# Sliding-window attention and channel mix: contiguous q/k evacuation, batch 0 attention pipelined, batch 1 attention inside tile 0

## The chip, the cores and the metric

One core of one Trainium2 chip. Times are device microseconds (us) of whole executions. A profiled execution has its own span, about 2 us under the time. Stages are compared in the profiled executions, totals in the timed ones.

Engines: PE is the matmul engine, PEld its weight loads, DVE the vector engine, ACT the scalar engine, POOL the general engine that here issues the loads. PSUM is the memory into which this kernel has PE write its results (the pools with `space=PS`); copying a result out of it is its evacuation. The identity is the matrix that the PE transposes of this kernel take as an operand. "L184" is line 184 of the kernel of that run.

## The reference, cut to what matters

```python
# q, k, v: (batch 8, heads 8, seq 576, dim 64), fp32
# heads 0-3: causal window of 32; heads 4-7: causal window of 128, every 4th position
scores = where(mask, q @ k^T / 8, -1e9); attn = softmax(scores); a = attn @ v
x = a as (8, 576, 512)                      # heads side by side
x_prev = x shifted by one position
xk = mu_k * x + (1 - mu_k) * x_prev;  xr = mu_r * x + (1 - mu_r) * x_prev
k = relu(xk @ w_k)                          # 512 -> 1024
out = sigmoid(xr @ w_r) * ((k * k) @ w_v)   # 1024 -> 512
```

## The kernel before: the parts that matter

The work per batch is: load, transpose q and k on PE (six steps `step_T`, each evacuated from PSUM by ACT), six attention blocks (`step_S` scores and exp, `step_P` weighted values and normalisation, `step_X` transposes of the result), then the "lerps" on DVE that make `xk` and `xr`. The dense part runs in nine tiles of 512 rows, each of 20 groups: 8 K, 4 R, 8 halves of V.

The plain heads' evacuation puts four interleaved phases r into one row, so it writes every fourth fp16 element:

```python
p_xo = ctx.enter_context(tc.tile_pool(name="p_xo", bufs=1, space=PS))   # one buffer
p_tb = ctx.enter_context(tc.tile_pool(name="p_tb", bufs=1, space=PS))   # one buffer

def step_T(b, n):
    ...
    if g == 0:      # plain heads: QKp
        for wi, w in enumerate(ws):
            o = QKp[b % 2][:, w, :, PAD:].rearrange("p h (j r) -> p h r j", r=R)[:, :, :, j0:j0 + nj]
            nc.scalar.activation(out=o, in_=tv[:, wi].rearrange("p (h r) x -> p h r x", h=2), func=AF.Copy)
    else:           # dilated heads: QKd, rows written contiguously
        ...
```

`step_T` 0 to 3 handle 96 rows (two of them plain, 128x768 each); steps 4 and 5 handle 48 rows (two 128x384 evacuations each).

The order of work, with the schedule of PE, ACT, DVE and POOL fixed by hand:

```python
load_batch(0)
make_identity(nc, ident)
... # weights w_k, w_r, w_v
load_batch(1)
...
for n in range(6): step_T(0, n)
fix_v(0)                                   # DVE copies 32 halo rows of v
for i in range(NB):                        # batch 0, block after block
    step_S(0, i); step_P(0, i, 0); step_P(0, i, 1)
    if i % 2 == 1: step_X(0, i // 2)
step_lerp_d(0); step_lerp(0, 0); step_lerp(0, 1)
scale_wv()                                 # DVE scales the value weights
for tt in range(NTT):
    if tt + 2 < B: load_batch(tt + 2)
    gs = moe_groups(tt)
    plan = attn_plan(tt + 1)               # S, P, X, lerps of batch tt+1, T of batch tt+2
    if tt == 0: plan = {}
    for g, f in enumerate(gs):             # a group, then the steps planned at it
        f()
        for a in plan.get(g, []): a()
    if tt == 0:                            # tile 0: batch 1 comes after the dense part
        for n in range(6): step_T(1, n)
        fix_v(1)
        plan = attn_plan(1)
        for g in range(20):
            for a in plan.get(g, []): a()
```

In `attn_plan`, S of block i stands at group 2i, its two P at 2i+2 and 2i+3, X after every second block, the lerps at 15, 16 and 18, the next transposes at 5, 9, 13, 15, 17 and 18, and `fix_v` at 19.

The softmax here doesn't subtract the row's maximum and nothing guards it: scores larger than these inputs give would overflow.

Of the kernel before, what the change touches and what calls it, by code (L numbers as in the profile page):

```python
# [10 lines left out]
AF = mybir.ActivationFunctionType  # L11
# [5 lines left out]
def kernel(  # L17
# [12 lines left out]
    nc = tc.nc  # L30
    B, H, S, D = q.shape
# [13 lines left out]
    lerp_p = ctx.enter_context(tc.tile_pool(name="lerp_p", bufs=1))  # L45
    xkp = ctx.enter_context(tc.tile_pool(name="xkp", bufs=3))
    k2p = ctx.enter_context(tc.tile_pool(name="k2p", bufs=2))
    outp = ctx.enter_context(tc.tile_pool(name="outp", bufs=3))
    PS = bass.MemoryType.PSUM
    p_mm = ctx.enter_context(tc.tile_pool(name="p_mm", bufs=4, space=PS))  # L50
    p_ps = ctx.enter_context(tc.tile_pool(name="p_ps", bufs=1, space=PS))
# [42 lines left out]
    def load_batch(b):  # L94
        for jc in range(2):
            load_qk(b, jc)
        load_v(b)

    ident = const.tile([128, 128], FP16)
    load_batch(0)  # L100
    make_identity(nc, ident)
    for i in range(2):
        nc.vector.memset(QKp[i][:, :, :, 0:PAD], 0.0)
        nc.vector.memset(QKd[i][:, :, :, 0:PAD], 0.0)
# [43 lines left out]
        nc.gpsimd.dma_start(out=wk[:, c], in_=moe_w_k[c * 128:(c + 1) * 128, :])  # L148
    for c in range(4):
        nc.gpsimd.dma_start(out=wr[:, c], in_=moe_w_r[c * 128:(c + 1) * 128, :])  # L150
    for c in range(8):
        nc.gpsimd.dma_start(out=wv[:, c], in_=moe_w_v[c * 128:(c + 1) * 128, :])
    load_batch(1)

    def scale_wv():
        for c in range(8):
# [5 lines left out]
    def step_T(b, n):  # L162
        jc, g, w1 = T_STEPS[n]
        j0, nj = JC[jc]
        t = ld[(b, jc)]
        tb = p_tb.tile([128, 768], FP16, name="tb")
        ws = (0, 1) if w1 is None else (w1,)
        nw = len(ws)
        tv = tb.rearrange("p (w s x) -> p w s x", w=nw, s=8)
        for wi, w in enumerate(ws):  # L170
            for sl in range(8):
                if g == 0:
                    hp, r = sl // 4, sl % 4
                    for par in range(2):
                        nc.tensor.transpose(out=tv[par * D:(par + 1) * D, wi, sl, :],  # L175
                                            in_=t[:nj, w, 2 * hp + par, r * D:(r + 1) * D], identity=ident[:nj, :nj])
                else:
                    h, rp = sl // 2, sl % 2
                    nc.tensor.transpose(out=tv[:, wi, sl, :], in_=t[:nj, w, 4 + h, rp * 2 * D:(rp + 1) * 2 * D],  # L179
                                        identity=ident[:nj, :nj])  # L180
        if g == 0:
            for wi, w in enumerate(ws):
                o = QKp[b % 2][:, w, :, PAD:].rearrange("p h (j r) -> p h r j", r=R)[:, :, :, j0:j0 + nj]
                nc.scalar.activation(out=o, in_=tv[:, wi].rearrange("p (h r) x -> p h r x", h=2), func=AF.Copy)  # L184
        else:
            for wi, w in enumerate(ws):
                o = QKd[b % 2][:, w, :, PAD:].rearrange("p h (a j) -> p h a j", a=2)[:, :, :, j0:j0 + nj]
                nc.scalar.activation(out=o, in_=tv[:, wi].rearrange("p (h a) x -> p h a x", h=4), func=AF.Copy)  # L188
# [4 lines left out]
    def step_S(b, i):  # L193
        ps = p_ps.tile([128, 2, 512], FP32, name="ps")
        for sl in range(4):
            for par in range(2):
                ho = par * 64
                if sl < 2:
                    lhsT = QKp[b % 2][ho:ho + 64, 1, sl, QB * i:QB * i + 128]
                    rhs = QKp[b % 2][ho:ho + 64, 0, sl, PAD + QB * i:PAD + QB * (i + 1)]  # L200
                else:
                    h, ii = 2 * (i % 2) + sl - 2, i // 2
                    lhsT = QKd[b % 2][ho:ho + 64, 1, h, QB * ii:QB * ii + 128]
                    rhs = QKd[b % 2][ho:ho + 64, 0, h, PAD + QB * ii:PAD + QB * (ii + 1)]
                nc.tensor.matmul(out=ps[:, par, sl * QB:(sl + 1) * QB], lhsT=lhsT, rhs=rhs, start=True, stop=True)  # L205
        at = AT[at_n[0] % 3]
        at_n[0] += 1
        nc.scalar.activation(out=at[:, :, :, 0:QB],  # L208
                             in_=ps[:, :, 0:4 * QB].rearrange("p a (s x) -> p a s x", s=4),
                             func=AF.Exp, scale=0.125)  # L210
        nc.vector.tensor_tensor(out=at[:, :, :, 0:QB], in0=at[:, :, :, 0:QB], in1=MK[combos[i]], op=ALU.mult)  # L211
        at_of[(b, i)] = at

    def step_P(b, i, g):
        at = at_of[(b, i)]
        rec = xp.tile([128, 4], FP32, name=f"rec{g}")
        x16 = xp.tile([128, 4, D], FP16, name=f"x16{g}", bufs=4)
        xo_of[(b, i, g)] = x16
        if g == 0:
            xo = p_xo.tile([128, 4, D + 1], FP32, name="xo")  # L220
            for hl in range(4):
                nc.tensor.matmul(out=xo[:, hl], lhsT=at[:, hl % 2, hl // 2, :], rhs=VAp[b % 2][:, i, hl, :],  # L222
                                 start=True, stop=True)
            nc.vector.reciprocal(out=rec[:QB], in_=xo[:QB, :, D])
            nc.vector.tensor_tensor(out=x16[:QB], in0=xo[:QB, :, 0:D],
                                    in1=rec[:QB].unsqueeze(2).to_broadcast([QB, 4, D]), op=ALU.mult)
        else:

            xo = p_xo.tile([128, 2, 2 * D + 2], FP32, name="xo")
            for hl in range(2):  # L230
                for par in range(2):
                    o = (2 * (i % 2) + hl) * (2 * D + 1) + par * (D + 1)
                    nc.tensor.matmul(out=xo[:, hl, par * (D + 1):(par + 1) * (D + 1)], lhsT=at[:, par, 2 + hl, :],
                                     rhs=VAd[b % 2][:, i // 2, o:o + D + 1], start=True, stop=True)
            rv = rec.rearrange("p (h a) -> p h a", h=2)
            nc.vector.reciprocal(out=rv[:QB], in_=xo[:QB, :, 0:2 * D + 2:2 * D + 1])
            nc.vector.tensor_tensor(out=x16[:QB].rearrange("p (a h) d -> p h a d", a=2),  # L237
                                    in0=xo[:QB, :, 1:2 * D + 1].rearrange("p h (a d) -> p h a d", a=2),
                                    in1=rv[:QB].unsqueeze(3).to_broadcast([QB, 2, 2, D]), op=ALU.mult)
# [32 lines left out]
    def step_lerp_d(b):  # L272
        xT = xT_of[b]
        dx = lerp_p.tile([128, 4, S], FP16, name="dx")
        nc.vector.tensor_tensor(out=dx[:, :, J:S], in0=xT[:, :, J:S], in1=xT[:, :, 0:S - J], op=ALU.subtract)
        nc.vector.tensor_tensor(out=dx[:, :, 1:J], in0=xT[:, :, 1:J], in1=xT[:, :, 3 * J:S - 1], op=ALU.subtract)
        nc.vector.tensor_copy(out=dx[:, :, 0:1], in_=xT[:, :, 0:1])
        xT_of[(b, "dx")] = dx
# [64 lines left out]
            gs.append(lambda ts=ts: step_V(tt, ts, 1))  # L343
        return gs

    def attn_plan(b):
        plan = {}
        if b >= B:
            return plan

        def at(g, f):
            plan.setdefault(g, []).append(f)
        for i in range(NB):
            at(2 * i, lambda i=i: step_S(b, i))
            at(2 * i + 2, lambda i=i: step_P(b, i, 0))
            at(2 * i + 3, lambda i=i: step_P(b, i, 1))
            if i % 2 == 1:
                at(2 * i + 4, lambda i=i: step_X(b, i // 2))
        at(15, lambda: step_lerp_d(b))
        at(16, lambda: step_lerp(b, 0))  # L360
        at(18, lambda: step_lerp(b, 1))
        if b + 1 < B:
            for n, g in enumerate((5, 9, 13, 15, 17, 18)):
                at(g, lambda n=n: step_T(b + 1, n))
            at(19, lambda: fix_v(b + 1))
        return plan

    with tc.manual_schedule(engines={ET.PE, ET.Activation, ET.DVE, ET.Pool}):
        for n in range(6):
            step_T(0, n)  # L370
        fix_v(0)
        for i in range(NB):
            step_S(0, i)
            step_P(0, i, 0)
            step_P(0, i, 1)
            if i % 2 == 1:
                step_X(0, i // 2)
        step_lerp_d(0)
        step_lerp(0, 0)
        step_lerp(0, 1)  # L380
        scale_wv()
        for tt in range(NTT):
            if tt + 2 < B:
                load_batch(tt + 2)
            gs = moe_groups(tt)
            plan = attn_plan(tt + 1)
            if tt == 0:
                plan = {}
            for g, f in enumerate(gs):
                f()  # L390
                for a in plan.get(g, []):
                    a()
            if tt == 0:
                for n in range(6):
                    step_T(1, n)
                fix_v(1)
                plan = attn_plan(1)
                for g in range(20):
                    for a in plan.get(g, []):
                        a()  # L400


# [28 lines left out]
```

## Time and profile before

353.17 us, median of 2 runs (352.47 to 353.86). The span of the profiled run is 351.4 us.

| stage (first K matmul to first K matmul) | us |
|---|---|
| prologue, to the first K matmul of tile 0 | 57.07 |
| tile 0 with batch 1 attention and transposes of batches 1 and 2 | 62.40 |
| tiles 1 to 6 | 192.21 |
| tiles 7 and 8 (dense only) | 39.72 |

The page of the kernel before, part 2: each digit is the busy share of one of 40 equal slices in tenths; PEclk is the granted PE clock in tenths.

```profile
span 351.4 us, 6171 instructions
...
PE   0134435973444697978788788878877977999994
...
ACT  6352331536453567567756757676677566425441
...
PEclk9999999996555589999999999999999999999999
```

PE is thin twice: in the first seven slices, and again from the tenth to the fourteenth, after the dense burst of tile 0. In the second gap its clock falls too. The table by stage for the kernel before says the same in numbers (columns: window, length, busy us and instruction count of each engine, granted clock, DMA share, GB/s); the third line is the stage with the transposes and attention of batch 1 and the transposes of batch 2 and no dense work, the last one a steady tile:

```profile
core 0: us, PE busy (x) PEld busy (x) DVE busy (x) ACT busy (x) POOL busy (x), PEclk, DMA share, GB/s
0.00:57.07 57.07, 14.91 (x217) 10.98 (x218) 22.44 (x87) 22.05 (x30) 35.69 (x63) 1.00 1.51 140
57.07:75.50 18.43, 18.43 (x78) 8.04 (x78) 9.84 (x23) 7.06 (x12) 0.00 (x0) 1.00 0.10 32
75.50:119.47 43.97, 19.19 (x316) 15.17 (x314) 16.97 (x40) 22.56 (x27) 9.69 (x14) 0.56 0.50 59
119.47:311.68 192.21, 159.72 (x1682) 81.12 (x1681) 136.84 (x317) 124.85 (x192) 31.04 (x46) 0.98 0.46 68
...
190.53:223.15 32.62, 26.68 (x297) 13.83 (x297) 23.24 (x54) 21.97 (x34) 8.14 (x12) 1.00 0.60 82
```

The evacuations of the transpose tile in the kernel before (smallest, median and largest duration in ns; first and last start; the shapes):

```profile
L184 ACT ACTIVATE QKp<-tb x32: 1023/1499/1878, 14.6 to 281.9; 128x768 f16<-128x768 f16 x16, 128x384 f16<-128x384 f16 x16
L188 ACT ACTIVATE QKd<-tb x32: 484/652/812, 20.2 to 284.1; 128x768 f16<-128x768 f16 x16, 128x384 f16<-128x384 f16 x16
L258 ACT ACTIVATE xT<-tb x24: 491/491/492, 35.0 to 307.0; 128x384 f16<-128x384 f16 x24
```

L184 and L188 move the same sizes; the strided one takes 1878 ns for what takes the other 812. L258 reads PSUM in steps of four elements and writes contiguously, and is as fast as a contiguous copy.

Who waited (us in total, times, longest), the kernel before:

```profile
PE tb L179 <- ACT QKp L184: 14.9, 10, 2.0
PE tb L253 <- ACT QKp L184: 13.9, 12, 2.0
PE tb L175 <- POOL ident masks.py:199: 13.7, 1, 13.7
...
PE tb L175 <- ACT QKp L184: 3.9, 2, 2.0
```

And where these waits sit in a steady tile: those of PE's instructions that waited for the evacuation or the mask, in order of time (start, duration, in brackets the idle time before and what ended it; three waits of 0.5 to 0.8 us for DVE's normalisation are cut). One period runs from the first line to the last.

```profile
190.51 0.30 PE L222 MATMUL xo<-VAp,AT 128*128 128x65 f16 x4 [0.81 <-DVE AT L211]
...
197.85 0.20 PE L253 MATMUL tb<-ident,x 96*128 96x96 f16 x1 [1.00 <-ACT QKp L184]
...
205.62 0.20 PE L253 MATMUL tb<-ident,x 96*128 96x96 f16 x1 [1.00 <-ACT QKp L184]
...
217.84 0.55 PE L179 MATMUL tb<-ident,qk 48*128 48x48 f16 x16 [1.01 <-ACT QKp L184]
223.15 0.30 PE L222 MATMUL xo<-VAp,AT 128*128 128x65 f16 x4 [0.81 <-DVE AT L211]
```

Three waits of 1 us for the strided evacuation: two before an X transpose, one before the last transpose step. The period ends with a wait for the mask multiplication on DVE.

### The profile page before, as it was taken

How to read it: one execution, taken by the hardware profiler on the slowest of the kernel's cores; microseconds unless marked ns; L12 is line 12 of the kernel's file. 1: busy time of each engine (PE TensorE's matmuls, PEld its weight loads, DVE VectorE, ACT ScalarE, POOL GpSimd, SP SyncE). 2: the span in 40 equal slices, each digit the busy share in tenths (PEclk: the TensorE clock that was granted, in tenths of full speed). 3: DMA queues.
4: the chain of work that ended last, by engine and by line, in shares of the span. 5: the costliest groups of instructions: out<-in, count | busy, mean ns of one | idle time of the engine just before them, and what ended most of it. 6: DMA issues, size and time to landing. Idle time of an engine off the chain costs nothing.

```text
span 351.4 us, 6171 instructions
## 1 busy us (share of the span) xinstructions
PE 247.3 (70%) x2448; PEld 130.9 (37%) x2448; DVE 202.7 (58%) x493; ACT 190.5 (54%) x285; POOL 76.4 (22%) x123
## 2 busy tenths in 40 slices
PE   0134435973444697978788788878877977999994
PEld 0132221433333343434443444444434433444441
DVE  3133339430433965596579658855966697695331
ACT  6352331536453567567756757676677566425441
POOL 7767432001105400540071017004100000000000
PEclk9999999996555589999999999999999999999999
DMA  8999996033705920795099019904710120111312
GB/s 105 133 175 196 118 131 52 9 112 40 97 2 33 138 33 2 88 147 89 30 100 195 2 32 142 151 2 76 83 33 20 42 60 2 48 44 59 93 30 90
DMA packets 56638, 26.62 MB, mean 76 GB/s; under 512 B 31521, under 2 KB 51489, under 8 KB 56609
## 3 DMA queue, kind: packets, MB, share of 16 engines
q0 software_dynamic: 49920, 16.78, 49.0%
q1 hardware_dynamic: 6688, 9.45, 9.2%
q8 instruction: 19, 0.31, 0.4%
q14 instruction: 11, 0.08, 0.1%
HBM read 33.56 MB, written 9.44 MB: 122 GB/s over the span
## 4 chain that ended last, share of the span: by engine, by line
PE 43%; ACT 27%; DVE 21%; issue 5%; DMA 2%; POOL 1%; DVEq 0%; ACTq 0%; POOLq 0%
ACT QKp L184 12%; PE mm L324 12%; PE mm L304 10%; PE mm L313 5%; ACT AT L208 5%; DVE AT L211 4%; PE tb L179 4%; DVE x L237 3%; PE xo L222 3%; PE tb L175 3%; ACT xT L258 2%; DMA qk<-in_k_dram 2%; DVE k L308 2%; PE ps L205 2%; DVE md L284 2%
## 5 line engine op out<-in xcount | busy, mean ns | idle before, releaser
L304 PE MATMUL mm<-xk,wk 128*128 128x512 f16 x288 | 74.1, 397 | 5.7 <-DVE xk L292 5.6
L324 PE MATMUL mm<-wv,k 128*128 128x512 f16 x288 | 71.8, 380 | 0.0
L307 ACT ACTIVATE kr<-mm 128x512 f16<-128x512 f32 x72 | 43.1, 604 | 33.8 <-PE mm L304 27.2
L211 DVE TENSOR_TENSOR AT<-AT,mk 128x768 f16<-128x768 f16 x48 | 26.8, 558 | 46.9 <-ACT AT L208 46.8
L184 ACT ACTIVATE QKp<-tb 128x768 f16<-128x768 f16 (+1 forms) x32 | 45.0, 1474 | 16.2 <-PE tb L175 16.1
L208 ACT ACTIVATE AT<-ps 128x768 f16<-128x768 f32 x48 | 39.1, 814 | 24.3 <-PE ps L205 24.3
L75 POOL DMA_DIRECT2D VAp<-in_v_dram x32 | 23.1, 727 | 115.7 <-PE xo L222 114.9
L308 DVE TENSOR_TENSOR k<-kr 128x512 f16<-128x512 f16 x72 | 30.0, 425 | 18.7 <-ACT kr L307 18.1
L328 DVE SCALAR_TENSOR_TENSOR ot<-sg,mm 128x512 f32<-128x512 f32 x36 | 24.7, 686 | 26.3 <-PE mm L324 26.3
L304 PEld LDWEIGHTS <-wk 128*128 128x128 f16 x288 | 26.1, 101 | 36.3 <-issue 10.5
L316 ACT ACTIVATE sg<-mm 128x512 f32<-128x512 f32 x36 | 21.7, 602 | 30.4 <-PE mm L313 28.0
L222 PE MATMUL xo<-VAp,AT 128*128 128x65 f16 x192 | 15.7, 208 | 32.0 <-DVE AT L211 16.1
L313 PE MATMUL mm<-wr,xr 128*128 128x512 f16 x144 | 37.0, 379 | 0.0
L188 ACT ACTIVATE QKd<-tb 128x768 f16<-128x768 f16 (+1 forms) x32 | 20.0, 650 | 28.7 <-PE tb L179 28.7
L324 PEld LDWEIGHTS <-k 128*128 128x128 f16 x288 | 24.9, 98 | 24.6
L175 PE MATMUL tb<-ident,qk 48*64 48x48 f16 (+1 forms) x512 | 16.3, 214 | 20.3 <-POOL ident masks.py:199 13.7
L179 PE MATMUL tb<-ident,qk 96*128 96x96 f16 (+1 forms) x256 | 15.0, 211 | 18.1 <-ACT QKp L184 14.9
L222 PEld LDWEIGHTS <-AT 128*128 128x128 f16 x192 | 10.1, 106 | 45.8 <-DVE x L237 25.2
L253 PE MATMUL tb<-ident,x 96*128 96x96 f16 x96 | 13.3, 222 | 15.0 <-ACT QKp L184 13.9
L175 PEld LDWEIGHTS <-qk 48*64 48x64 f16 (+1 forms) x512 | 13.6, 124 | 24.0 <-issue 14.1
L284 DVE TENSOR_TENSOR md<-dx,murep 128x2304 f16<-128x2304 f16 x16 | 21.7, 1355 | 0.3
L258 ACT ACTIVATE xT<-tb 128x384 f16<-128x384 f16 x24 | 11.8, 491 | 18.5 <-PE tb L255 18.4
(53 smaller groups left out, 309.3 us busy)
## 6 DMA issues: line engine op xcount, KB each, us to landing
qk<-in_q_dram POOLq DMA_DIRECT2D x8, 384.0 KB, 6.4
qk<-in_k_dram POOLq DMA_DIRECT2D x8, 384.0 KB, 7.7
VAp<-in_v_dram POOLq DMA_DIRECT2D x32, 72.0 KB, 4.6
out_dram<-ot SPq DMA_DIRECT2D x8, 256.0 KB, 2.5
out_dram<-ot SPq DMA_DIRECT2D x8, 224.0 KB, 2.4
qk<-in_q_dram POOLq DMA_DIRECT2D x8, 192.0 KB, 7.6
qk<-in_k_dram POOLq DMA_DIRECT2D x8, 192.0 KB, 7.6
VAd<-in_v_dram POOLq DMA_DIRECT2D x16, 96.0 KB, 4.6
```

The costliest lines, as they stand in the source:

```text
L175: nc.tensor.transpose(out=tv[par * D:(par + 1) * D, wi, sl, :], in_=t[:nj, w, 2 * hp + par, r * D:(r + 1) * D], identity=ident[:nj, :nj])
L179: nc.tensor.transpose(out=tv[:, wi, sl, :], in_=t[:nj, w, 4 + h, rp * 2 * D:(rp + 1) * 2 * D], identity=ident[:nj, :nj])
L184: nc.scalar.activation(out=o, in_=tv[:, wi].rearrange("p (h r) x -> p h r x", h=2), func=AF.Copy)
L208: nc.scalar.activation(out=at[:, :, :, 0:QB], in_=ps[:, :, 0:4 * QB].rearrange("p a (s x) -> p a s x", s=4), func=AF.Exp, scale=0.125)
L211: nc.vector.tensor_tensor(out=at[:, :, :, 0:QB], in0=at[:, :, :, 0:QB], in1=MK[combos[i]], op=ALU.mult)
L222: nc.tensor.matmul(out=xo[:, hl], lhsT=at[:, hl % 2, hl // 2, :], rhs=VAp[b % 2][:, i, hl, :], start=True, stop=True)
L284: nc.vector.tensor_tensor(out=md, in0=dx, in1=murep[:, w], op=ALU.mult)
L304: nc.tensor.matmul(out=pk, lhsT=wk[:, c, f * 128:(f + 1) * 128], rhs=xk_t[tt][:, c], start=(c == 0), stop=(c == 3))
L307: nc.scalar.activation(out=kr, in_=pk, func=AF.Relu, scale=8.0)
L308: nc.vector.tensor_tensor(out=k2_of[tt][:, f], in0=kr, in1=kr, op=ALU.mult)
L313: nc.tensor.matmul(out=pr, lhsT=xr_t[tt][:, c, ts * 128:(ts + 1) * 128], rhs=wr[:, c], start=(c == 0), stop=(c == 3))
L324: nc.tensor.matmul(out=pv, lhsT=k2_of[tt][:, f, ts * 128:(ts + 1) * 128], rhs=wv[:, f], start=(f == 0), stop=(f == 7))
```

## The change

Its intent: evacuate with contiguous writes (the stride moves to the PSUM read), start the first transposes before all loads are issued, pipeline batch 0 attention, and run batch 1 (transposes among the K groups, attention among the R and V groups) inside tile 0 instead of after it. For that, batch 1 is loaded ahead of the value weights, whose scaling moves into tile 0.

```diff
-    outp = ctx.enter_context(tc.tile_pool(name="outp", bufs=3))
+    outp = ctx.enter_context(tc.tile_pool(name="outp", bufs=4))
     ...
+    make_identity(nc, ident)
     load_batch(0)
-    make_identity(nc, ident)
     ...
+    load_batch(1)
     for c in range(8):
         nc.gpsimd.dma_start(out=wv[:, c], in_=moe_w_v[c * 128:(c + 1) * 128, :])
-    load_batch(1)
     ...
-                o = QKp[b % 2][:, w, :, PAD:].rearrange("p h (j r) -> p h r j", r=R)[:, :, :, j0:j0 + nj]
-                nc.scalar.activation(out=o, in_=tv[:, wi].rearrange("p (h r) x -> p h r x", h=2), func=AF.Copy)
+                o = QKp[b % 2][:, w, :, PAD + R * j0:PAD + R * (j0 + nj)].rearrange("p h (j r) -> p h j r", r=R)
+                nc.scalar.activation(out=o, in_=tv[:, wi].rearrange("p (h r) x -> p h x r", h=2), func=AF.Copy)
     ... # attn_plan becomes attn_steps, t_steps and merge(steps, groups); same positions
-        for i in range(NB):
-            step_S(0, i); step_P(0, i, 0); step_P(0, i, 1); ...      # (cut) block after block
-        scale_wv()
+        merge(attn_steps(0), [])
         for tt in range(NTT):
             ...
             if tt == 0:
-                ... # all groups, then step_T(1, .), fix_v(1), attn_plan(1)
+                gs = gs[:8] + [gs[8 + 3 * n] for n in range(4)] + [gs[9 + 3 * n + m] for n in range(4) for m in range(2)]
+                for g in range(8):
+                    gs[g]()
+                    if g >= 2:
+                        step_T(1, g - 2)
                 fix_v(1)
+                steps = attn_steps(1) + t_steps(2, (9, 11, 13, 15, 17, 18))
+                gs = gs[8:]
+                steps.append((3, scale_wv))
+            else:
+                steps = attn_steps(tt + 1) if tt + 1 < B else []
+                if tt + 2 < B:
+                    steps += t_steps(tt + 2, (5, 9, 13, 15, 17, 18))
+            merge(steps, gs)
```

(Here the cuts are marked with "...", and statements of several lines are joined by semicolons.) The fourth buffer of `outp` belongs to the new order of tile 0, where all four R groups come before the first V group. In tiles 1 to 8 the order of instructions on PE and DVE stays as it was; only the evacuation differs.

More of the change, by code (lines that the diff above doesn't have):

```diff
@@ L344, in moe_groups, with attn_steps, merge, t_steps @@
         return gs
-    def attn_plan(b):
-        plan = {}
-        if b >= B:
-            return plan
-        def at(g, f):
-            plan.setdefault(g, []).append(f)
-        for i in range(NB):
-            at(2 * i, lambda i=i: step_S(b, i))
-            at(2 * i + 2, lambda i=i: step_P(b, i, 0))
-            at(2 * i + 3, lambda i=i: step_P(b, i, 1))
-            if i % 2 == 1:
-                at(2 * i + 4, lambda i=i: step_X(b, i // 2))
-        at(15, lambda: step_lerp_d(b))
-        at(16, lambda: step_lerp(b, 0))
-        at(18, lambda: step_lerp(b, 1))
-        if b + 1 < B:
-            for n, g in enumerate((5, 9, 13, 15, 17, 18)):
-                at(g, lambda n=n: step_T(b + 1, n))
-            at(19, lambda: fix_v(b + 1))
-        return plan
+    def attn_steps(b):
+        steps = []
+        for i in range(NB):
+            steps.append((2 * i, lambda i=i: step_S(b, i)))
+            steps.append((2 * i + 2, lambda i=i: step_P(b, i, 0)))
+            steps.append((2 * i + 3, lambda i=i: step_P(b, i, 1)))
+            if i % 2 == 1:
+                steps.append((2 * i + 4, lambda i=i: step_X(b, i // 2)))
+        steps.append((15, lambda: step_lerp_d(b)))
+        steps.append((16, lambda: step_lerp(b, 0)))
+        steps.append((18, lambda: step_lerp(b, 1)))
+        return steps
+    def merge(steps, groups):
+        plan = {}
+        for pos, f in steps:
+            plan.setdefault(pos, []).append(f)
+        last = max(list(plan) + [len(groups) - 1])
+        for g in range(last + 1):
+            if g < len(groups):
+                groups[g]()
+            for f in plan.get(g, []):
+                f()
+    def t_steps(b, at):
+        st = [(g, lambda n=n: step_T(b, n)) for n, g in enumerate(at)]
+        st.append((at[-1] + 1, lambda: fix_v(b)))
+        return st
     with tc.manual_schedule(engines={ET.PE, ET.Activation, ET.DVE, ET.Pool}):
@@ L371 @@
         fix_v(0)
-        for i in range(NB):
-            step_S(0, i)
-            step_P(0, i, 0)
-            step_P(0, i, 1)
-            if i % 2 == 1:
-                step_X(0, i // 2)
-        step_lerp_d(0)
-        step_lerp(0, 0)
-        step_lerp(0, 1)
-        scale_wv()
+        merge(attn_steps(0), [])
         for tt in range(NTT):
+            gs = moe_groups(tt)
             if tt + 2 < B:
                 load_batch(tt + 2)
-            gs = moe_groups(tt)
-            plan = attn_plan(tt + 1)
             if tt == 0:
-                plan = {}
-            for g, f in enumerate(gs):
-                f()
-                for a in plan.get(g, []):
-                    a()
-            if tt == 0:
-                for n in range(6):
-                    step_T(1, n)
-                fix_v(1)
-                plan = attn_plan(1)
-                for g in range(20):
-                    for a in plan.get(g, []):
-                        a()
+                gs = gs[:8] + [gs[8 + 3 * n] for n in range(4)] + [gs[9 + 3 * n + m] for n in range(4) for m in range(2)]
[3 more added lines that the diff above has]
+                        step_T(1, g - 2)
+                fix_v(1)
+                steps = attn_steps(1) + t_steps(2, (9, 11, 13, 15, 17, 18))
[6 more added lines that the diff above has]
+            merge(steps, gs)
 _INS = ['q', 'k', 'v', 'moe_mu_k', 'moe_mu_r', 'moe_w_k', 'moe_w_v', 'moe_w_r']
```

## The prediction

> **What bounds the kernel now.** The span is 351.4 us and no engine bounds all of it: PE is busy 70%, DVE 58%, ACT 54%. By the chain of waits it falls into stages:
> - 0 to 57 us, serial prologue. The first transposes start at 13.7, after the identity (waits view: PE idle 13.7 us for it), although the first q load landed at 7.1. Transposes of batch 0 end at 27.4; its attention, block after block (3.5 to 5 us each), ends in lerps, and the first K matmul is at 57.1.
> - 57 to 75.5: tile 0, dense matmuls.
> - 75.5 to 119.5: batch 1 attention and batch 2 transposes with no dense work beside them; PE is busy 44%, its clock 0.56 (table by stage).
> - 119.5 to 284.5: tiles 1 to 5, then period 32.6 us, PE busy 82%; tile 6 takes 27.2, tiles 7 and 8 39.7.
>
> **Plain q/k evacuation.** It takes 1.88 us for 128x768 (4-element steps in the write); the dilated one, same size with contiguous rows, 0.81. The Trainium skill, "ScalarE: Activation LUTs", section "What ACT_TABLE_LOAD costs", gives 186 ns + 0.833 ns per element, 826 ns here; the dilated evacuation agrees. The stride moves to the PSUM read; the xT copy that reads PSUM in 4-element steps costs 0.49 us for 384, as much as contiguous ones, so I expect no penalty: 0.81 and 0.49 us for 1.88 and about 1.0. That is about 25 us of ACT off 190. In a steady tile PE stands about 1.0 us three times for it (two X transposes, one transpose step). The third is covered, since DVE runs without a gap from the lerps to the next tile's first mask. So about 1.9 us per tile, estimated, not 3: period 30.7; five tiles give 9.5 us.
>
> **Prologue.** Transposes can start at about 7.3, but ACT builds the mu tiles until 10.1, so the first evacuation gains 4.5 us, the shorter evacuations about 3 more. Pipelining hides S behind mask and normalisation; with a single xo buffer a block still costs about 3.2 us (P, S, exp 0.82, mask 0.57, normalise 0.64), 3.6 with X; it saves about 3 us. First K: about 46.5, 10.5 earlier.
>
> **Tile 0.** K matmuls with batch 1 transposes take about 13 us; then attention 1 with the other 12 groups inside it, about 18 us from first to last P, weight scaling (1.7 us of DVE) included; the tail with lerps about 8.5. Tile 1 starts at about 89 instead of 119.5: 30.5 us gained in all, 20 of it here. Batch 1 loads come earlier, the value weights later (about 45 us, needed near 60); neither should wait.
>
> **Rest.** Tiles 6 to 8 unchanged (67 us). The sum: 30.5 + 9.5 + 1 to 2 from a less cold tile 1; span 309, wall 311 us.
>
> **Predicted: 311 us, 8 in 10 within 304 to 319.** Faster by over 2%: 0.97; within: 0.02; slower: 0.01.
>
> **Signs of it.** Plain evacuation mean about 0.65 (both sizes); PE waits on QKp, 33 us over three groups, nearly gone; first K at 45 to 48; tile 1 at 86 to 92; period 30 to 31.5; DVE gapless around tile boundaries; last two tiles 39.7.
>
> **What would make it wrong.** A slow strided PSUM read (evacuation above 1.2 us: about 12 us worse). Period down by the full 3 us (305), if DVE is not the limit. A cold clock in the sparse tail of tile 0 ("TensorE: Matmul & The Clock Gate", part 1: an idle window brings half clock; here 0.56 in the attention-only stage): 2 to 4 us. Late value weights or batch 2 loads would show as DMA waits in tile 0.

## The result and the profile after

309.98 us, median of 2 runs (309.28 to 310.67), against 353.17. The ratio of the two is 0.8777, 95% interval 0.8665 to 0.8889. Ratios here are the mean time of one kernel's fast runs over that of the other's of the same rounds, so not quite the ratio of the medians.

| stage | before | after | difference | predicted |
|---|---|---|---|---|
| prologue | 57.07 | 44.66 | -12.4 | -10.5 |
| tile 0 | 62.40 | 42.19 | -20.2 | -20 |
| tiles 1 to 6 | 192.21 | 180.65 | -11.6 | -10.5 to -11.5 |
| tiles 7 and 8 | 39.72 | 39.70 | 0.0 | 0 |
| span | 351.4 | 307.2 | -44.2 | |

Tile by tile, tile 1 falls by 4.26 us (34.49 to 30.23), tiles 2 to 5 by 2.07 each, and tile 6 grows by 0.99 (27.22 to 28.21): its longer wait for the mask (1.81 us, 0.81 before) comes after its first K matmul, where the stages are cut. Tile 1's gain came with the evacuation (30.32 in e1, with the thin stage still in front of it; 33.79 in e2, merged but with the strided evacuation), not with the merged tile 0.

The page of the changed kernel, part 2:

```profile
span 307.2 us, 6179 instructions
...
PE   0344529978389897989798979897989788999994
...
ACT  5643316944457655765575557555755564262530
...
PEclk9999999999769999999999999999999999999998
```

The thin stretch after tile 0 has gone except for one slice, and the stretch of low clock has shrunk from five slices to two. The table by stage, the changed kernel, same cuts as above:

```profile
0.00:44.66 44.66, 14.55 (x216) 11.00 (x217) 21.85 (x87) 18.80 (x30) 31.21 (x57) 1.00 1.66 145
44.66:86.85 42.19, 33.45 (x393) 18.59 (x392) 25.57 (x63) 22.93 (x39) 14.31 (x21) 0.92 1.08 105
86.85:267.50 180.65, 158.15 (x1682) 80.18 (x1681) 137.22 (x317) 109.62 (x192) 30.94 (x46) 0.99 0.50 74
...
122.03:152.59 30.56, 26.62 (x297) 13.73 (x297) 23.15 (x54) 18.93 (x34) 8.11 (x12) 1.00 0.76 103
```

In the steady tile ACT does 3.0 us less (21.97 to 18.93), but the period falls by only 2.06 us (32.62 to 30.56). PE and DVE do the same work as before.

The evacuations in the changed kernel, and the first waits for QKp that are left:

```profile
L184 ACT ACTIVATE QKp<-tb x32: 485/640/811, 9.8 to 237.4; 128x768 f16<-128x768 f16 x16, 128x384 f16<-128x384 f16 x16
L188 ACT ACTIVATE QKd<-tb x32: 485/648/811, 13.2 to 238.9; 128x768 f16<-128x768 f16 x16, 128x384 f16<-128x384 f16 x16
```

```profile
PE tb L179 <- ACT QKp L184: 2.8, 3, 1.0
PE tb L175 <- ACT QKp L184: 2.7, 1, 2.7
```

The two evacuations now cost the same to within 1 ns at the ends, so a PSUM read in 192-byte steps (the 128x768 ones) is free on ACT here, and the strided write was the whole cost. Waits for QKp fell from 32.7 us to 5.5.

The missing microsecond per tile: PE's waits for the mask in the changed kernel, one period apart,

```profile
122.03 0.30 PE L222 MATMUL xo<-VAp,AT 128*128 128x65 f16 x4 [1.82 <-DVE AT L211]
...
152.59 0.30 PE L222 MATMUL xo<-VAp,AT 128*128 128x65 f16 x4 [1.82 <-DVE AT L211]
```

and DVE just before it, from the end of the X evacuation to the mask ("..." marks lines cut):

```profile
142.45 1.06 DVE L275 TENSOR_TENSOR dx<-xT 128x1728 f16<-128x1728 f16 x1 [1.53 <-ACT xT L265]
...
144.48 1.35 DVE L284 TENSOR_TENSOR md<-dx,murep 128x2304 f16<-128x2304 f16 x1
145.86 1.43 DVE L292 TENSOR_TENSOR xk<-md,xT 128x1280 f16<-128x1280 f16 x2
...
150.77 0.49 DVE L90 COPY VAp<-VAp 32x1300 f16<-32x1300 f16 x1
151.19 0.42 DVE L92 COPY VAd<-VAd 32x1034 f16<-32x1034 f16 x1
151.64 0.42 DVE L308 TENSOR_TENSOR k<-kr 128x512 f16<-128x512 f16 x1
151.98 0.55 DVE L211 TENSOR_TENSOR AT<-AT,mk 128x768 f16<-128x768 f16 x1
```

Of these lines and the cut ones only the first has a bracket: from its start DVE is busy 9.91 of the 10.08 us to the mask's end. The wait of 1.01 us for the third evacuation disappeared, and the wait for the mask grew by the same 1.01 us, from 0.81 to 1.82.

### The profile page after: what moved, and what is told of

The parts are those of the page before. It is cut to its first block, busy times and chain, and to the rows that moved or that the text cites. A ratio compares the mean times of both kernels' runs of the same rounds, so it can differ in the third digit from the quotient of the medians.

```text
span 307.2 us, 6179 instructions
## 1 busy us (share of the span) xinstructions
PE 241.2 (78%) x2448; PEld 125.4 (41%) x2448; DVE 201.2 (65%) x493; ACT 165.4 (54%) x285; POOL 76.5 (25%) x123
## 3 DMA queue, kind: packets, MB, share of 16 engines
q1 hardware_dynamic: 6688, 9.45, 10.5%
## 4 chain that ended last, share of the span: by engine, by line
PE 43%; DVE 29%; ACT 16%; issue 5%; DMA 4%; POOL 1%; DVEq 0%; POOLq 0%; ACTq 0%
PE mm L304 13%; PE mm L324 12%; ACT AT L208 5%; PE mm L313 5%; DVE md L284 5%; DVE AT L211 5%; DVE x L237 4%; PE xo L222 3%; DVE ot L328 3%; ACT xT L265 3%; DVE xk L292 3%; PE tb L175 3%; DMA qk<-in_k_dram 3%; ACT xT L258 3%; ACT kr L307 3%
## 5 line engine op out<-in xcount | busy, mean ns | idle before, releaser
L222 PE MATMUL xo<-VAp,AT 128*128 128x65 f16 x192 | 15.0, 202 | 30.3 <-DVE x L237 18.5
L175 PE MATMUL tb<-ident,qk 48*64 48x48 f16 (+1 forms) x512 | 15.3, 207 | 11.6 <-DMA qk<-in_q_dram 7.1
L184 ACT ACTIVATE QKp<-tb 128x768 f16<-128x768 f16 (+1 forms) x32 | 19.9, 648 | 8.3 <-PE tb L175 8.0
L83 POOL DMA_DIRECT2D VAd<-in_v_dram x32 | 19.9, 625 | 11.0 <-DMA qk<-in_k_dram 6.3
L225 DVE TENSOR_TENSOR x<-xo,rec 96x256 f16<-96x256 f32 x48 | 20.2, 420 | 1.7
L237 DVE TENSOR_TENSOR x<-xo,rec 96x256 f16<-96x256 f32 x48 | 20.2, 420 | 1.6
```

Source lines behind the costliest of these rows:

```text
L175: nc.tensor.transpose(out=tv[par * D:(par + 1) * D, wi, sl, :], in_=t[:nj, w, 2 * hp + par, r * D:(r + 1) * D], identity=ident[:nj, :nj])
L222: nc.tensor.matmul(out=xo[:, hl], lhsT=at[:, hl % 2, hl // 2, :], rhs=VAp[b % 2][:, i, hl, :], start=True, stop=True)
L237: nc.vector.tensor_tensor(out=x16[:QB].rearrange("p (a h) d -> p h a d", a=2), in0=xo[:QB, :, 1:2 * D + 1].rearrange("p h (a d) -> p h a d ...
```

## The experiments

Twelve kernels. "Before" ran beside each call: 353.36, 353.43 and 353.77 us. The changed kernel ran beside none of them, and e9 to e12 ran on another chip, so totals are best compared by their ratios to before. All were correct.

| run | us (lowest to highest) | ratio to before (95% interval) |
|---|---|---|
| e1: before, contiguous evacuation only | 332.79 (332.68 to 334.29) | 0.9434 (0.9392 to 0.9477) |
| e2: changed, strided evacuation | 328.29 (327.18 to 328.92) | 0.9289 (0.9254 to 0.9325) |
| e3: changed, strided for 96 rows only | 326.55 (324.64 to 328.68) | 0.9245 (0.9184 to 0.9307) |
| e4: changed, strided for 48 rows only | 312.17 (311.00 to 313.02) | 0.8834 (0.8799 to 0.8870) |
| e5: changed, identity late | 314.30 (313.17 to 315.75) | 0.8895 (0.8865 to 0.8926) |
| e6: changed, batch 0 attention serial | 315.04 (314.81 to 317.41) | 0.8929 (0.8894 to 0.8964) |
| e7: changed, batch 1 after tile 0 | 323.45 (323.10 to 324.65) | 0.9158 (0.9135 to 0.9180) |
| e8: changed, old load order | 309.37 (308.42 to 309.86) | 0.8744 (0.8723 to 0.8766) |
| e9: changed, halo copies inside the tile | 307.01 (306.78 to 307.66) | 0.8683 (0.8665 to 0.8701) |
| e10: changed, mask built early | 308.62 (308.20 to 308.96) | 0.8725 (0.8707 to 0.8743) |
| e11: changed, weight scaling spread | 308.59 (306.87 to 310.85) | 0.8731 (0.8702 to 0.8759) |
| e12: e9, e10 and e11 together | 305.65 (304.11 to 306.00) | 0.8634 (0.8611 to 0.8658) |

The theory: each part of the change acts in its own stage, and in the steady tiles only the evacuations before the X transposes are on the path, because DVE bounds the tile boundary. The rivals: every microsecond of ACT saved counts; or the reordering did it all.

### e1 and e2: the evacuation alone, and all but the evacuation

```diff
 # e1: this edit on the kernel before; e2: its reverse on the changed kernel
-                o = QKp[...][:, w, :, PAD:].rearrange("p h (j r) -> p h r j", r=R)[:, :, :, j0:j0 + nj]
-                ... in_=tv[:, wi].rearrange("p (h r) x -> p h r x", h=2)
+                o = QKp[...][:, w, :, PAD + R * j0:PAD + R * (j0 + nj)].rearrange("p h (j r) -> p h j r", r=R)
+                ... in_=tv[:, wi].rearrange("p (h r) x -> p h x r", h=2)
```

> The kernel before with only the contiguous evacuation. Theory (part of the evacuation time is on the path): steady period 30.5 us instead of 32.6 (about 10 us over tiles 1 to 5), about 3 us each in the transposes of batch 0, batch 1 and batch 2, which nothing covers there: 332 to 337 us. Rival A (all 25 us of ACT time counts): 328. Rival B (the reordering brought it all, the evacuation little): above 345.

> The changed kernel with the strided evacuation put back. Theory: period back at 32.6 us (10 us over five tiles), first K matmul about 3 us later, 4 to 6 us in tile 0: 326 to 330 us. Rival A (all 25 us count): 335. Rival B: below 315.

Measured: 332.79 and 328.29 us, both inside the theory's ranges and outside the rivals'. The evacuation alone is worth 20.6 us on the kernel before, about 18 on the changed one. By stage, from the first K matmuls:

| stage | e1 against before | e2 against after |
|---|---|---|
| prologue | 53.76: -3.3 | 47.01: +2.35 |
| tile 0 | 56.48: -5.9 | 46.08: +3.9 |
| tiles 1 to 6 | 180.77: -11.4 | 192.29: +11.6 |

In tiles 1 to 6 the evacuation explains everything, with or without the rest of the change. In tile 0 it is worth less once batch 1 has dense groups beside it: part of it is then hidden. Taken in the other order, the rest of the change is worth 16.3 us in tile 0 with the strided evacuation (62.40 to 46.08, e2).

### e3 and e4: which evacuations are on the path

```diff
+                if jc == 0:      # e3;   e4: if jc == 1:
+                    ... # the strided pair of lines of before
+                else:
                     ... # the contiguous pair
```

> The changed kernel with the strided write put back only for the 96-row part (two evacuations of 768 per batch, the ones before the X transposes). Theory: nearly all of the evacuation's worth in the steady tiles sits here: period 32.5 us, total 322 to 327. Rival (each us of ACT counts alike): 2.1 us a batch, 8 batches, 327, and period 32.6.

> The changed kernel with the strided write put back only for the 48-row part (two evacuations of 384 per batch, near the end of a tile). Theory (DVE is the limit at the tile boundary, this wait is covered): period stays 30.5 us, PE's wait for the first mask of the next block shrinks by about 1 us as the wait for the evacuation comes back; only batches 0 to 2 pay, total 310.5 to 313. Rival (every us of evacuation counts): 1 us a batch, period 31.5, total 317 to 318.

Measured: 326.55 and 312.17 us. In e3 the rival's range holds the total too; e3 alone would not decide. e4 does: 312.17, not 317 to 318. Its PE, as in the timelines above (line numbers are four higher than in the changed kernel):

```profile
123.73 0.30 PE L226 MATMUL xo<-VAp,AT 128*128 128x65 f16 x4 [0.80 <-DVE AT L215]
...
148.99 0.56 PE L179 MATMUL tb<-ident,qk 48*128 48x48 f16 x16 [1.01 <-ACT QKp L185]
...
154.28 0.30 PE L226 MATMUL xo<-VAp,AT 128*128 128x65 f16 x4 [0.80 <-DVE AT L215]
```

The period is 154.28 - 123.73 = 30.55 us, as without the slow evacuation. The wait for the evacuation is back at 1.01 us, and the wait for the mask is 0.80 instead of 1.82. The two add up to the same: PE waits for DVE either way, and the third evacuation only decides under which name. In e3 the period is 32.63 us, all of before's. The 2 us of e4's total came outside the steady tiles: 0.2 in the prologue, 1.0 in tile 0, 0.5 in tiles 1 to 6.

### e5: the identity late

```diff
-    make_identity(nc, ident)
     load_batch(0)
+    make_identity(nc, ident)
```

> The changed kernel with the identity built after the loads are issued, as before. Theory: the first transposes start at about 13.7 us again instead of 7.1, but the mask tiles (done at about 21.2 us) already held the first block back, so only about 3.5 us are lost: 313 to 314.5. Rival A (all of the 6.6 us counts): 316.5. Rival B (loads bound the prologue): 310.

Measured: 314.30 us, in the theory's range; the first K matmul came at 48.91, 4.25 us later. That is more than the 3.5 that I expected and less than the 6.6 that the first transposes move: the first evacuation moves by 5.04 us (9.80 to 14.84), as in the changed kernel it has to wait for ACT's mu tiles, and the first P by 4.22 (21.68 to 25.90), as there the masks had held it back. (The profiled run of e5 had one tile 1.3 us longer than its neighbours, so its total is not used.)

### e6: batch 0 attention block after block

```diff
-        merge(attn_steps(0), [])
+        for i in range(NB):
+            step_S(0, i); step_P(0, i, 0); step_P(0, i, 1)
+            if i % 2 == 1: step_X(0, i // 2)
+        step_lerp_d(0); step_lerp(0, 0); step_lerp(0, 1)
```

> The changed kernel with batch 0 attention block after block, as before. From the first mask to the lerp took 24.6 us before and 19.3 after, so theory: about 5 us lost, 314.5 to 316. Rival (as I predicted, pipelining is worth 3): 313.

Measured: 315.04 us; first K matmul at 50.44, 5.8 us later. Of these, 0.6 are not the edit's: in this run the first k load landed later (the second transpose step starts at 11.46, not 10.64), and the first P came at 22.25, not 21.68. From there to the first K matmul it took 28.19 us against 22.98, so pipelining is worth 5.2. PE in e6, then in the changed kernel:

```profile
22.25 0.40 PE L222 MATMUL xo<-VAp,AT 128*128 128x65 f16 x4 [2.51 <-DVE AT L211]
...
50.44 4.63 PE L304 MATMUL mm<-xk,wk 128*128 128x512 f16 x12 [5.16 <-DVE xk L292]
```

```profile
21.68 0.40 PE L222 MATMUL xo<-VAp,AT 128*128 128x65 f16 x4 [2.77 <-DVE AT L211]
...
44.66 4.97 PE L304 MATMUL mm<-xk,wk 128*128 128x512 f16 x12 [5.16 <-DVE xk L292]
```

The prediction's 3 us was too low. Identity (4.25), pipelining (5.2) and evacuation (2.35), each undone alone, add up to 11.8 of the 12.4 us gained in the prologue. They are not independent: the evacuation alone is worth 3.3 there on the kernel before (e1).

### e7: batch 1 after the dense part of tile 0

```diff
+        scale_wv()                       # before the tiles, as in the kernel before
         ...
             if tt == 0:
-                ... # reordered groups, step_T(1, .) among the K groups
+                for g in range(20): gs[g]()
+                for n in range(6): step_T(1, n)
                 fix_v(1)
+                gs = []
+                steps = attn_steps(1) + t_steps(2, (5, 9, 13, 15, 17, 18))
```

> The changed kernel with tile 0 dense first and batch 1 transposes, attention and batch 2 transposes after it. Theory: first K at 44.7 as in the changed kernel, tile 1 starts 14 to 17 us later (at 101 to 104), a half clock stage comes back, total 323 to 328. Rival (it was mostly the shorter evacuation that shortened this stage): tile 1 at most 8 us later, total below 318.

Measured: 323.45 us. Tile 0 starts and tile 1 starts, in e7:

```profile
44.72 9.21 PE L304 MATMUL mm<-xk,wk 128*128 128x512 f16 x32 [5.16 <-DVE xk L292]
...
100.79 1.89 PE L304 MATMUL mm<-xk,wk 128*128 128x512 f16 x4
```

The start of tile 0 is unmoved, tile 1 comes 13.9 us later than in the changed kernel (86.85), a little under the 14 that I gave as the least. The granted clock of the attention-only stage is 0.59 again. So the merge is worth about 14 us where the evacuation is already contiguous; the other 6 of the 20 gained in tile 0 are the evacuation's (e1: 5.9).

### e8: the old load order

```diff
-    load_batch(1)
     for c in range(8):
         nc.gpsimd.dma_start(out=wv[:, c], in_=moe_w_v[c * 128:(c + 1) * 128, :])
+    load_batch(1)
```

> The changed kernel with the value weights issued before batch 1 again. Theory: batch 1 q/k then land at about 36 us and v at about 45, ahead of their use at 49.6 and 57, so nothing changes: 309 to 311. Rival (the load order is needed for the merged tile 0): a DMA wait before the batch 1 transposes or the first P, over 2 us, 312 or more.

Measured: 309.37 us, the same as the changed kernel; in tile 0 only POOL's issue of loads waits for DMAs, and twice a weight load of PE for the v loads (1.3 us in all); the matmuls show no such wait. Moving batch 1's loads ahead was not needed.

### e9: the halo copies away from the tile boundary

If DVE bounds the boundary, taking 0.91 us of DVE work out of it must shorten the period.

```diff
     def t_steps(b, at):
         ...
-        st.append((at[-1] + 1, lambda: fix_v(b)))
+        st.append((11, lambda: fix_v(b)))
```

> The changed kernel with the two halo copies of the next-but-one batch (0.91 us of DVE) moved from the tile boundary to group 11. Theory (DVE, gapless from the lerps to the first mask, sets the boundary): PE's wait for that mask falls from 1.82 to about 0.9 us, the period from 30.55 to about 29.7, six boundaries, total 304.5 to 307. Rival (PE or ACT sets the period, DVE only follows): period stays 30.5, total 309 to 311.

Measured: 307.01 us. In the profiled run:

```profile
122.82 0.30 PE L222 MATMUL xo<-VAp,AT 128*128 128x65 f16 x4 [0.83 <-DVE AT L211]
...
152.77 0.30 PE L222 MATMUL xo<-VAp,AT 128*128 128x65 f16 x4 [0.83 <-DVE AT L211]
```

The wait falls from 1.82 to 0.83 us as the theory says, and the period by 0.61 us, to 29.95: no other engine's work changed, so DVE was the limit. It is not the full 0.99 because the copies are not free inside the tile. From the first P of a tile to the first lerp is 20.42 us in the changed kernel (122.03 to 142.45) and 20.80 in e9 (122.82 to 143.62): 0.38 us are given back there. Of the total I had expected 304.5 to 307, so it is just beyond the poor end. Tile 0 (42.58 against 42.19) and tile 1 (31.74 against 30.23) were longer in the profiled run. Tile 1 had the lower clock for longer (0.50 against 0.73 between 88 and 92 us); whether that is due to the edit was not tested.

### e10: the mask built earlier

```diff
-    load_batch(0)
+    for jc in range(2):
+        load_qk(0, jc)
+    m01 = ...            # memset and four selects on POOL, moved up unchanged
+    load_v(0)
```

> The changed kernel with the mask's building on POOL issued ahead of the v loads. Theory: in the changed kernel the first exp ends at about 19.8 us but its masking ends at 21.6 because the mask copies on DVE run until 21.2; with the copies done by then, the first P matmul comes 1 to 1.3 us earlier and so does all that follows: total 308.4 to 309.2. Rival (v for the first P lands late, or the loads set it): no change, 309.5 to 310.5.

Measured: 308.62 us. The first P matmul of the changed kernel, then of e10:

```profile
21.68 0.40 PE L222 MATMUL xo<-VAp,AT 128*128 128x65 f16 x4 [2.77 <-DVE AT L211]
```

```profile
20.82 0.40 PE L224 MATMUL xo<-VAp,AT 128*128 128x65 f16 x4 [1.94 <-DVE AT L213]
```

It came 0.86 us earlier, a little less than the 1 to 1.3 expected, and the first K matmul 0.84 us earlier (43.82). The total alone does not settle it (the interval overlaps that of e8); these starts do. Building the masks, hidden in the kernel before, had come onto the path once the transposes started early.

### e11: the value weights scaled in pieces

```diff
                     if g >= 2:
                         step_T(1, g - 2)
+                    if g >= 4:
+                        scale_wv((2 * g - 8, 2 * g - 7))
-                steps.append((3, scale_wv))
```

> The changed kernel with the value weight scaling spread over the K groups 4 to 7 of tile 0, two chunks each, in place of one piece of 1.7 us inside the attention. Theory: PE's wait of 1.2 us for the scaled weights goes and the attention of batch 1 loses its 1.7 us hole on DVE: total 307 to 309, period unchanged. Rival (the K phase is then slowed by as much, or the weights land too late): 309.5 or more.

Measured: 308.59 us, 306.87 to 310.85; the median is in the theory's range, but the spread is as wide as the effect. The profile is clearer. PE's wait of 1.18 us for the scaled weights, present in the changed kernel, is gone; tile 0 takes 40.42 us in place of 42.19. In the same run the first k load came later (the second transpose step waits for it until 11.32, against 10.64) and with it the first K matmul (45.41), so the total shows less.

### e12: the three together

The three edits above in one kernel.

> The three edits together: halo copies inside the tile, mask early, scaling spread. Theory: they act in different stages and add up, 7 to 9 us less than the changed kernel: 301 to 303.5. If one only moves a wait that another also removes, the sum falls short: 304 or more.

Measured: 305.65 us (304.11 to 306.00), ratio 0.8634 (0.8611 to 0.8658). It beats both kernels: its interval lies below that of e8 (0.8723 to 0.8766), which ran as fast as the changed kernel and is better measured. The gain over the changed kernel is about 1.4% (305.65 against 309.98), and short of the 7 to 9 us that I expected. In the profiled run it is 0.8 us in the prologue (43.83), 0.9 in tile 0 (41.25) and 2.8 in tiles 1 to 6 (177.86 against 180.65). The halo copies cost part of their gain inside the tiles, as in e9, and tile 0 keeps less of the spread scaling than e11 showed. What takes the rest in tile 0 was not isolated.

## Why the prediction was right, point by point

- **Total.** 311 predicted, 309.98 measured. The split by stage held within 2 us, and no stage gained less than predicted, so the stages' errors do not cancel (inside the prologue two do in part, below): 30.5 predicted to the start of tile 1, 32.6 measured; 10.5 to 11.5 predicted after it, 11.6 measured.
- **Evacuation.** 0.81 and 0.49 us predicted, 0.811 and 0.485 measured. The Trainium skill, "ScalarE: Activation LUTs", section "What ACT_TABLE_LOAD costs", gives 186 ns + 0.833 ns per element, which makes an estimate of 826 and 506 ns: the trace is 2% and 4% under it. The argument that carried it was in the trace of before: another copy already read PSUM with a stride at no cost.
- **Two of three waits count in the steady tile.** Predicted 1.9 us per tile, measured 2.06; e4 and e9 show why the third does not, from both sides. With a slower third evacuation the period stays; with less DVE work at the boundary it falls.
- **Prologue.** The term that was mis-sized is "it saves about 3 us" for pipelining: undone, it costs 5.2 us between the first P and the first K matmul (e6). I had costed a block at 3.2 us, 3.6 with X. The chain of waits shows the exps of the changed kernel's blocks 2.9 to 3.4 us apart (22.55, 25.43, 28.65, 31.53, 34.92), against 3.4 to 5.1 before. "About 3 more" for the shorter evacuations came out as 2.35 (e2), since the prediction had missed the masks: ready at 21.16, they now hold back the first block, by 0.86 us (e10). The first K matmul at 44.66 missed "45 to 48" by a hair.
- **Tile 0.** 20 predicted, 20.2 measured; tile 1 at 86.85, inside 86 to 92. The merge is worth 13.9 (e7), the evacuation the rest; in the other order 16.3 and 3.9 (e2).
- **Waits for loads.** "Neither should wait" held for the loads (in tile 0 only POOL's own issue waits for a DMA), but PE did wait 1.18 us for the scaling of the value weights on DVE, which I had put into the sum as DVE time, not as a stall.
- **Cold clock.** It did fall to 0.50, from tile 0's tail into tile 1 (about 80 to 90 us). The clock page of the Trainium skill, "TensorE: Matmul & The Clock Gate", part 1, has the clock fall after at least one idle window of about 3.4 us; PE's longest idle time in the 10 us before was 1.50 us (up to 78.08), so the trace shows the fall without a gap of that length. Its cost was not isolated. The first K matmul of tile 1 (86.85) came 0.07 us after the lerp that it needs (xk ends at 86.78), but also just as PE ended the last transposes of batch 2 (86.12, 0.80 us long). Both chains end there, and no run shows which of them was the limit.

## What to carry to other kernels

A wait that goes away is worth only the difference to the next one behind it: before crediting it, look whether the engine behind the following wait is idle anywhere in between. If it is gapless, the saved time comes back under another name. For this stage without dense work, moving dense groups into it paid more than shortening its links, 14 us against 6 (16 against 4 in the other order). After such a move, setup work that used to be hidden (masks, weight scaling) is the next thing to check.

## What the Trainium skill lacked or had wrong

- "ScalarE: Activation LUTs", section "What ACT_TABLE_LOAD costs", has one rate per element and no word on strided fp16 writes to SBUF. Here a write in 8-byte steps cost 2.23 ns per element ((1878 - 1023) / 384), a contiguous one 0.85 ((811 - 485) / 384).
- "SBUF — State Buffer", section "Door 1: The DMA port swizzle", lets bf16, a 2-byte type, stride up to 8 elements for free. ACT's write of fp16, also 2 bytes, with a stride of 4 elements was 2.3 times as long as the contiguous one (1878 against 812 ns).
- "PSUM — Partial Sum Buffer", section "Specifications (TRN2)", warns of non-contiguous patterns for matmuls and does not say what a strided read by ACT costs. Here an ACT read of PSUM in 192-byte steps cost nothing (811 ns, the same as contiguous rows).
- "TensorE: Matmul & The Clock Gate", part 4, says that the full clock does not engage for PE transposes. Here a step of 32 transposes took 0.69 us in stretches with a granted clock of 1.0 that also held dense matmuls, and 1.04 us at 0.50 (tile 0's tail): they do profit from it. Whether transposes alone would bring it about was not tested.
- The same page, section "Seeing it yourself", warns that the clock events in a trace can be unreliable. A case of it here: the same step took 1.05 us in the prologue, the time of the half clock, while the clock column shows 1.00 there.
